# One RWKV-attention and MoE kernel, one reordering: where the inverses, the loads, x and the MoE pieces stand in a hand-written step table

## The chip, the cores and the metric

The kernel runs on one core of a Trainium2 chip. The metric is device time in microseconds (us), the median of several runs. Engines are named as in the profile: PE is the matrix engine (PEld its weight loads), DVE, ACT and POOL are the three vector-like engines, SP is the engine that here does nothing but issue DMAs (SPq is its queue). Each engine works through its own instructions strictly in the order of the program; between engines there are only semaphores.

## The reference

For 4 batches and 8 heads a state of 40x40 is carried over 768 time steps; its output is the input of a mixture layer:

```
for t in range(S):
    y[:, :, t] = einsum('bhd,bhde->bhe', rt, state)
    Sa = einsum('bhde,bhe->bhd', state, at)
    state = state * wt[:, :, None, :] - Sa (x) bt + vt (x) kt
x = y as (B, S, 320);  x_prev = x shifted by one time step
xk = mu_k * x + (1 - mu_k) * x_prev
xr = mu_r * x + (1 - mu_r) * x_prev
out = sigmoid(xr @ w_r) * (max(xk @ w_k, 0)**2 @ w_v)
```

All of it is float32. w_k is 320x1024, w_v 1024x320, w_r 320x320.

## The kernel before, in words

**Chunks.** Time is cut into 12 chunks of 64 (index k). Inside a chunk the recurrence becomes products, and one triangular system per head, whose 32x32 diagonal blocks are inverted on POOL. A chunk is done in two halves p = 0, 1 of 16 heads each; names such as `psc0` and `psc1` carry the half.

**What one chunk goes through.** `w` loads w, a, b, k of a half into the tile `wab` (L274); there are two such buffers, so a load waits until the transposes `pkt` of the half before the last are done with it. `Q` or `q` checks a half: ACT squares `wab` into `pe` (L289), an instruction that must wait for the load. The front (`F`, L300) then has four stages on DVE: two scans, two products into `az`, one product back into `wab`. `psc` (L322) makes the score matrix `sn` on PE, copied by ACT. `to` (L359) writes the blocks of `sn` to a DRAM scratch `tx` in 128-byte runs; `tl` (L373) loads them back as `ta` with one block per partition and inverts all of them on POOL (about 60 small instructions, L384 and L387) into `td`; `ts` (L364) stores `td` to the scratch `ty`; `tk` (L369) fetches `ty` back into `sn`. These trips to DRAM and back turn the layout around, each one must land before the next may be issued, and all are issued by SP. `tl` loads after `tx` has landed, `tk` after `ty` has.

**The chain of a chunk** (L403) has five stages on PE, `z T L U s`, each followed by ACT or DVE copies of its result `ch`; `T`, `L` and `U` need the fetched inverses in `sn`. `put`, `pmt`, `pgh`, `py` make the output y from the chain, from `r` and from `v` (`vr`, loaded by `r`, L397, two buffers; `vu`, loaded by `v`). `py` is copied by DVE into `xp`, and `x` (L512) sends `xp` by five DMAs into the tile `x` that the MoE layer reads.

**MoE work.** `Mix` (L115) cuts the layer of one chunk into 18 pieces: 8 products `ph` (relu, square and a split into two halves follow on ACT and DVE), 8 products `pv`, 2 products `pr` (each counted where its generator yields; the last two `pv` are the last two pieces). Before them stand 7 mixing steps on DVE and ACT (difference, three for xk, three for xr), the first four of which the first piece needs. `advance` (L527) issues the next piece; while a chunk's later pieces run, it may also issue mixing steps of the next chunk, if that chunk's `Mix` is already in the list, which happens at the end of its step (L635).

**Order.** The program is written out by hand (manual schedule): per chunk a step of 25 slots, `STEP` (L38). A slot's names are called from left to right; what they put off (`later`) comes at the end of that slot or of a following one. A name works on chunk k plus an offset (L568, L569): in step k, `psc`, `pkt`, `to`, `tl` belong to chunk k+2, `w` and `Q` to k+3, `ts` and `tk` to k+1, `r` and `v` to k+1, `x` to k. `M` is one MoE piece from step 1, slot 12 on (`MOE_FROM`); earlier it converts one of the 18 pieces of the weights from float64 bits (L222), which are loaded on ACT's queue. Slots are counted from 0. There are 19 slots with an `M` before.

**Head.** Ahead of step 0, chunks 0 and 1 (and half of 2) are brought through front, scores and inversion (L584 to L616).

In the step table the names from slot 14 on were, before:

```
"py0 tl", "M pgh1", "M pkt0", "M py1 w0 r0", "M pkt1 ts", "M w1 r1", "M", "M tk", "M x", "M Q0", "M F"
```

## Time and profile before

| | before |
|---|---|
| median of 3 runs (us) | 803.15 (802.92 to 803.17) |
| the profiled execution, own time (us) | 802.47 |
| its span in the profile (us) | 800.8 |
| busy share PE / DVE / ACT / POOL | 71% / 54% / 39% / 47% |
| mean granted clock of PE | 0.806 |
| DMA moved, mean rate | 71.15 MB, 89 GB/s |
| DMA packets, of them under 512 bytes | 120554, 96573 |

How to read the rows of the profile: a chain row is start, duration, what. A row of the timeline is start, duration, engine, line, operation, out<-in, shapes, count, and in brackets the idle time ahead of it and what ended it. A row of the windows is the stretch, its length, busy us (and instructions) of PE, PEld, DVE, ACT, POOL, then the granted clock of PE (1.00 is full), the mean busy share of the 16 DMA engines, and GB/s. An SPq row with a long duration is a DMA whose issue was itself held up.

### The profile page before, as it was taken

What the parts mean: (1) busy time and instruction counts of PE and PEld (TensorE: products, weight loads), DVE (VectorE), ACT (ScalarE), POOL (GpSimd) and SP (SyncE); (2) the same over time, 40 slices, a digit from 0 to 9 for tenths busy, and PEclk for the clock granted to TensorE, in tenths of its full rate; (3) what the DMA queues carried; (4) which work ended last, traced back from release to release, by engine and by line L of the source; (5) the groups of instructions that cost most, each with busy time, mean ns of one, the idle gap of its engine ahead of it and who ended that gap; (6) DMA issues with size and microseconds to landing.
All of it is one profiled execution on the core that took longest, in us unless ns stands there. A gap on an engine that the chain in (4) does not pass through costs nothing.

```text
span 800.8 us, 24776 instructions
## 1 busy us (share of the span) xinstructions
PE 571.1 (71%) x10658; PEld 516.7 (65%) x10658; DVE 433.5 (54%) x773; ACT 313.4 (39%) x793; POOL 373.5 (47%) x814
## 2 busy tenths in 40 slices
PE   1122086057979799797896794993994997988965
PEld 1122075046868688786786693883883886988965
DVE  7486677497466493663744544643653654232431
ACT  2122241143554464444443442442532533525333
POOL 4284787702823855858548248138038228200000
PEclk9999985555979789698698597597598598695979
DMA  4709536913625718348066066057048054160010
GB/s 122 152 13 188 125 72 148 187 40 69 132 50 133 128 35 182 53 108 154 23 129 113 23 134 110 21 121 138 6 100 156 9 102 74 30 102 10 10 33 20
DMA packets 120554, 71.15 MB, mean 89 GB/s; under 512 B 96573, under 2 KB 110869, under 8 KB 118149
## 3 DMA queue, kind: packets, MB, share of 16 engines
q1 hardware_dynamic: 118214, 63.74, 40.0%
q10 hardware_dynamic: 2223, 5.76, 2.9%
q8 instruction: 85, 1.39, 0.8%
q14 instruction: 32, 0.26, 0.1%
HBM read 52.98 MB, written 10.22 MB: 79 GB/s over the span
## 4 chain that ended last, share of the span: by engine, by line
PE 34%; DMA 28%; DVE 12%; SPq 9%; POOL 8%; issue 4%; ACT 3%; DVEq 0%; POOLq 0%; ACTq 0%
DMA ty<-td 10%; PE ph L112 9%; DMA ta<-tx 7%; PE pv L112 5%; SPq L371 4%; PE psc L333 4%; POOL td L387 3%; DMA x<-xp 3%; POOL ttmp L384 3%; PE ch L437 3%; PE ch L431 2%; PE ch L425 2%; SPq L521 2%; PE ch L419 2%; DMA wbuf<-in_w_v_dram 2%
## 5 line engine op out<-in xcount | busy, mean ns | idle before, releaser
L387 POOL TENSOR_TENSOR td<-td,ttmp 128x30 f32<-128x30 f32 (+4 forms) x360 | 165.3, 459 | 28.2
L384 POOL TENSOR_TENSOR ttmp<-ta,td 128x30 f32<-128x30 f32 (+4 forms) x360 | 161.2, 448 | 28.3
L112 PE MATMUL ph<-xk,wkh 120*128 120x256 f32 x480 | 115.5, 340 | 62.9 <-ACT xk L90 61.0
L112 PEld LDWEIGHTS ph<-xk,wkh 120*128 120x128 f32 x480 | 84.3, 223 | 72.7 <-ACT xk L90 64.7
L90 POOL TENSOR_TENSOR mc<-zs,pe 104x320 f32<-104x320 f32 x24 | 18.6, 790 | 172.1 <-DVE zs L90 171.9
L90 ACT ACTIVATE hf<-ph 128x256 f32<-128x256 f32 x96 | 36.9, 384 | 151.6 <-PE ph L112 150.9
L90 DVE TENSOR_TENSOR hl<-hf,hh 128x256 fp32r<-128x256 f32 x96 | 42.8, 445 | 92.0 <-ACT hh L90 91.7
L419 PE MATMUL ch<-zs,sn 32*32 32x40 f32 x768 | 29.9, 263 | 75.2 <-ACT zs L90 44.6
L378 POOL TENSOR_SCALAR_AFFINE_SELECT td<-ta 64x512 f32<-64x512 f32 x24 | 17.6, 732 | 139.5 <-DMA ta<-tx 139.2
L419 PEld LDWEIGHTS ch<-zs,sn 32*32 32x32 f32 x768 | 27.2, 164 | 78.6 <-ACT zs L90 44.9
L112 PE MATMUL ph<-xk,wkl 120*128 120x256 f32 x288 | 74.3, 316 | 0.1
L333 PE MATMUL psc<-az,wab 40*64 40x64 f32 x1536 | 37.9, 268 | 45.9 <-DVE wab L318 39.0
L112 PE MATMUL pv<-wvh,hh 128*128 128x320 f32 x192 | 69.5, 362 | 0.0
L333 PEld LDWEIGHTS psc<-az,wab 40*64 40x64 f32 x1536 | 34.1, 178 | 49.9 <-issue 48.8
L112 PE MATMUL pv<-wvh,hl 128*128 128x320 f32 x192 | 62.6, 326 | 0.0
L112 PE MATMUL pv<-wvl,hh 128*128 128x320 f32 x192 | 62.4, 325 | 0.0
L112 PEld LDWEIGHTS ph<-xk,wkl 120*128 120x128 f32 x288 | 57.2, 227 | 0.4 <-DMA xk<-xk 0.4
L90 DVE TENSOR_TENSOR az<-psc,mask 64x512 f32<-64x512 f32 x48 | 33.1, 689 | 41.5 <-PE psc L333 40.9
L90 ACT COPY vu<-ch 32x320 f32<-32x320 f32 x96 | 40.0, 416 | 27.5 <-PE ch L419 25.9
L139 DVE TENSOR_TENSOR diff<-x 120x256 f32<-120x256 f32 x36 | 16.6, 511 | 61.5 <-DMA x<-xp 61.4
L90 DVE TENSOR_TENSOR gh<-pgh,mask 128x512 f32<-128x512 f32 x48 | 30.9, 685 | 27.1 <-PE pgh L483 27.1
L306 DVE TENSOR_TENSOR_SCAN pe<-wab,first 104x520 f32<-104x520 f32 x24 | 31.6, 1318 | 23.8 <-ACT pe L90 19.7
(95 smaller groups left out, 1233.8 us busy)
## 6 DMA issues: line engine op xcount, KB each, us to landing
wab<-in_wab_dram SPq DMA_DIRECT2D x22, 835.7 KB
vr<-in_rvd_dram SPq DMA_DIRECT2D x24, 416.0 KB
ta<-tx SPq DMA_DIRECT2D x24, 256.0 KB
vu<-in_vt_dram SPq DMA_DIRECT2D x24, 256.0 KB
out_dram<-sig SPq DMA_DIRECT2D x48, 80.0 KB
tx<-sn SPq DMA_DIRECT2D x48, 64.0 KB
ty<-td SPq DMA_DIRECT2D x24, 128.0 KB
sn<-ty SPq DMA_DIRECT2D x48, 64.0 KB
```

The lines of the kernel that those rows point to most:

```text
L90: f(*args, **kw)
L112: nc.tensor.matmul(out, lhsT=left[i][g], rhs=right[j][g], start=start and k == 0, stop=stop and k == len(terms) - 1)
L139: nc.vector.tensor_tensor(out=d4[:, g], in0=x[:, g, :, 1:], in1=x[:, g, :, 0:C], op=ALU.subtract)
L306: nc.vector.tensor_tensor_scan(out=pe.rearrange("p x t -> p (x t)"), data0=w[:, 0:SP], data1=first, initial=0.0, op0=ALU.mult, op1=ALU.add)
L333: nc.tensor.matmul(to[64 * y:64 * y + 64, x], lhsT=kb[r0:r1, x, y], rhs=az[r0:r1, i, x], start=True, stop=True)
L371: nc.sync.dma_start(y, x)
L378: nc.gpsimd.affine_select(out=TD[h], in_=TA[h, i::2], compare_op=ALU.is_gt, fill=0.0, base=-i, pattern=[[-2, 16], [1, 32]], channel_multip ...
L384: nc.gpsimd.tensor_tensor(out=tmp, in0=TA[:, s:s + 1, s + 1:].broadcast_to([128, rows, n]), in1=TD[:, 0:rows, s:s + 1].broadcast_to([128, ...
L387: nc.gpsimd.tensor_tensor(out=TD[:, 0:rows, s + 1:], in0=TD[:, 0:rows, s + 1:], in1=tmp, op=ALU.subtract)
L419: mm(c3[a:a + 32, x], lhsT=sn[a:a + 32, x, 0:32], rhs=zs[a:a + 32, x], start=True, stop=True)
L425: mm(c3[a + 32:a + 64, x], lhsT=sn[a:a + 32, x, 32:64], rhs=vu[a:a + 32, i, x, 0:HD], start=False, stop=True, skip_group_check=True)
L437: mm(c3[r0:r1, x], lhsT=kt[:, i, x], rhs=vu[:, i, x, 0:HD], start=(x == 0), stop=True, skip_group_check=(x > 0))
```

## The change

Only the order of issue is changed; every instruction and every byte stays. In the step table:

- `ts` goes from slot 18 to 15 and `tk` from 21 to 18: both now stand ahead of the loads `w0` and `w1`, which go from 17 and 19 to 19 and 20.
- `x` goes from slot 22 to 19, behind `w0` and ahead of `w1`.
- `r0`, `r1` go from slots 17 and 19 of the step before (offset 1) to slots 1 and 3 of the chunk's own step (offset 0).
- `tl` goes from slot 14 to 13.
- `q1` goes from slot 1 to 3; the front of half 1 follows it in slots 4 to 7 instead of 3 to 6.
- Slot 18 loses its `M`: 18 slots with an `M` instead of 19.
- In the head, the loads of chunk 1 come behind `tri(0)`, `tri(1)` directly behind `tri_out(1)`, the load of `r` and `v` of chunk 0 by `load_rv` goes into step 0, store and fetch of chunk 0's inverses come between the two loads of chunk 2, and the eight weight pieces are spread 2, 2, 3, 1 instead of 1, 2, 2, 2, 1.

```
@@ -36,8 +36,8 @@
 MOE_FROM = (1, 12)
 
 STEP = [x.split() for x in (
-    "z0 z1 F", "M F q1", "T0 T1 F", "M pmt0 F", "L0 L1 F", "M pmt1 F", "U0 U1 F", "M psc0", "s0 s1", "M psc1", "M put0 to",
-    "M put1 v", "M pgh0", "M", "py0 tl", "M pgh1", "M pkt0", "M py1 w0 r0", "M pkt1 ts", "M w1 r1", "M", "M tk", "M x",
+    "z0 z1 F", "M F r0", "T0 T1 F", "M pmt0 q1 r1", "L0 L1 F", "M pmt1 F", "U0 U1 F", "M psc0 F", "s0 s1", "M psc1", "M put0 to",
+    "M put1 v", "M pgh0", "M tl", "py0", "M pgh1 ts", "M pkt0", "M py1", "pkt1 tk", "M w0 x", "M w1", "M", "M",
     "M Q0", "M F")]
 
 
@@ -565,7 +565,7 @@
                 psc(k, p)
 
             DO = dict(put=put, pmt=pmt, pgh=pgh, py=py)
-            AHEAD = dict(r=(1, load_rv), w=(3, load_wab), Q=(3, check), q=(2, check), psc=(2, scores), pkt=(2, pkt))
+            AHEAD = dict(r=(0, load_rv), w=(3, load_wab), Q=(3, check), q=(2, check), psc=(2, scores), pkt=(2, pkt))
             BOTH = dict(v=(1, load_v), to=(2, tri_out), tl=(2, tri), ts=(1, tri_store), tk=(1, tri_back), x=(0, send_x))
 
             def to_scores(k):
@@ -588,32 +588,30 @@
                     load_w(j, nc.sync)
                 to_scores(0)
                 tri_out(0)
-                load_wab(1, 0)
                 pkt(0, 1)
                 flush()
-                some_weights(1)
+                some_weights(2)
                 tri(0)
-                load_wab(1, 1)
+                for p in range(2):
+                    load_wab(1, p)
                 some_weights(2)
                 to_scores(1)
                 tri_out(1)
                 pkt(1, 1)
                 flush()
+                tri(1)
+                load_v(0)
                 load_wab(2, 0)
-                load_v(0)
-                for p in range(2):
-                    load_rv(0, p)
-                tri(1)
+                some_weights(3)
+                tri_store(0)
+                tri_back(0)
                 load_wab(2, 1)
                 for p in range(2):
-                    some_weights(2)
                     check(2, p)
                     flush()
                     for _ in range(2):
                         next(fronts[-1][2])
-                some_weights(1)
-                tri_store(0)
-                tri_back(0)
+                    some_weights(1 - p)
                 for k in range(NK):
                     chains = [chain(k, p) for p in range(2)]
                     for n, slot in enumerate(STEP):
```

## The prediction, on record before the changed kernel was run

> **What bounds the kernel now.** First the page of the profile: is one engine full all the time?

> ```profile
> span 800.8 us, 24776 instructions
> PE   1122086057979799797896794993994997988965
> PEclk9999985555979789698698597597598598695979
> ```

> From slice 9 on PE is nearly full twice and then half empty, about every 60 us, and the granted clock falls in the same rhythm. So a step is PE work, a hole, and a stretch at low clock behind the hole. The chain of waits and the timeline of PE give the beat; I take the start of stage T (L419) as the mark of a step and call it T(k). The first row below is T(2), from the timeline.

> ```profile
> 224.59 2.34 PE L419 MATMUL ch<-zs,sn 32*32 32x40 f32 x62 [0.38 <-DMA sn<-ty]
> ```

> ```profile
> 143.24 8.89 DMA wbuf<-in_w_v_dram
> 152.23 6.18 DMA wbuf<-in_w_v_dram
> ...
> 324.87 2.33 PE ch L419 x62
> ...
> 563.53 2.27 PE ch L419 x64
> ...
> 624.91 2.27 PE ch L419 x64
> ...
> 677.52 2.27 PE ch L419 x64
> ...
> 725.15 2.27 PE ch L419 x64
> ```

> The five later rows are T(4), T(8), T(9), T(10) and T(11). Steps 2 and 3 took (324.87 - 224.59) / 2 = 50.1 us each, step 8 took 61.4, steps 2 to 8 together (624.91 - 224.59) / 7 = 57.2 each, steps 9 and 10 52.6 and 47.6. The chain of waits through step 8 shows what stands in the hole:

> ```profile
> 583.07 1.09 PE psc L333 x64
> ...
> 588.45 5.64 DMA ta<-tx
> ...
> 598.60 8.91 DMA ty<-td
> ...
> 609.02 3.23 SPq L371
> ...
> 614.78 3.12 DMA x<-xp
> ...
> 617.92 1.44 DVE diff L139 x3
> ...
> 623.05 1.86 PE ph L112 x7
> ...
> 656.22 1.14 PE ph L112 x8
> ...
> 657.97 1.08 PE pv L112 x6
> ```

> The end runs through SP: scratch loaded, inverses stored, their fetch issued, x sent, mixed on DVE and ACT, and only then the first MoE piece of the new chunk, which stands in slot 1, ahead of T on PE. SP's own timeline shows the loads between:

> ```profile
> 596.63 0.35 SPq L277 DMA_DIRECT2D wab<-in_wab_dram  x1
> ...
> 601.44 3.40 SPq L277 DMA_DIRECT2D wab<-in_wab_dram  x1
> ...
> 607.59 4.66 SPq L371 DMA_DIRECT2D sn<-ty  x4
> ...
> 617.27 2.46 SPq L90 DMA_DIRECT2D out_dram<-sig  x4
> ```

> The windows show what the hole costs beyond itself:

> ```profile
> 608.00:612.00 4.00, 1.36 (x48) 1.24 (x44) 2.41 (x5) 0.85 (x2) 3.53 (x7) 1.00 0.94 164
> 612.00:616.00 4.00, 0.00 (x0) 0.00 (x0) 0.00 (x0) 0.00 (x0) 3.37 (x9) 0.59 1.03 147
> ...
> 636.00:640.00 4.00, 4.00 (x80) 3.58 (x79) 0.26 (x1) 2.19 (x6) 0.00 (x0) 0.50 0.00 0
> ...
> 644.00:648.00 4.00, 4.00 (x91) 3.48 (x89) 2.33 (x5) 2.34 (x6) 0.69 (x1) 1.00 0.20 32
> ```

> PE stops at about 609.4 and resumes at 623.05, a hole of 13.7 us; the clock is then 0.50 until after 640, some 17 us of work at half speed, that is 8 us more.

> **Part by part. 18 pieces a step.** A chunk's MoE layer has 18 pieces. Before, step 1 issued 12 from slot 12 on and left 6; each later step issues 19 and leaves one less, until step 7 leaves none and step 8 must begin slot 1 with a chunk whose x has only just been sent. After, step 1 issues 11 (slots 12, 13, 15 to 17, 19 to 24), 7 stay over, and stay 7: slots 1 to 11 work off the old chunk, the new one begins in slot 12, mixed long before. PE then reaches T without x. The price is at the end: 7 pieces more behind the last step, at 1.1 us (1.14 and 1.08 above) 7.8 us.

> **Store and fetch ahead of the loads, x too.** I count from the end of `psc1`, 583.07 + 1.09 = 584.16.

> ```profile
> wab<-in_wab_dram SPq DMA_DIRECT2D x22, 835.7 KB
> vr<-in_rvd_dram SPq DMA_DIRECT2D x24, 416.0 KB
> ```

> ```profile
> 600.00:604.00 4.00, 3.63 (x37) 3.18 (x35) 0.99 (x2) 2.19 (x6) 3.29 (x10) 1.00 0.84 197
> ```

> At 197 GB/s a `wab` load is 4.2 us, a `vr` load 2.1. `ta` was issued at +4.3; now the stores of the chunk whose last piece falls in slot 11 stand before it on SP (2.46), so +6.8, and it lands 5.64 later, +12.4. The store `ty` was landed at 598.60 + 8.91 = 607.51, 10.9 after the `wab` load was issued in front of it; without 6.3 of loads it is worth some 4.6 (an estimate from these rows), so it lands at +17.0, and the fetch, as many bytes, at +21.5. Then `w0` behind it in the DMA queues, +25.7; x, issued by about +24 and landing 3.1 later or behind `w0`, at +28; `w1` at +32. Before, fetch and x had both loads and both `r` ahead of them.

> PE needs no load to get from `psc1` to T: before, it issued 14 pieces and stage z and stood still at 609.4, +25.2; after, it is 13, z and one more in slot 1, the same. The fetch at +21.5 is no longer late. What is late next is `w0`: `Q0` in slot 23 makes ACT wait for it, and on ACT there are queued behind it the three passes of the piece in slot 24 and the copies of z.

> ```profile
> 606.08 0.72 ACT L90 ACTIVATE pe<-wab,limit 104x512 f32<-104x512 f32 x1
> ...
> 608.50 0.43 ACT L90 COPY zs<-ch 128x320 f32<-128x320 f32 x1 [1.61 <-PE ch L413]
> ```

> That is 0.72 + 3 x 0.4 + 0.43 = 2.3 behind +25.7: T at +28.0, PE idle 2.8 us instead of 13.7. From T to the end of `psc1`, step 4 had

> ```profile
> 342.29 1.16 PE L333 MATMUL psc<-az,wab 40*64 40x64 f32 x64
> ```

> and with T(4) of step 4 at 324.87 that is 18.6 us, partly at half clock, partly held by DVE. I take it whole, since x, at +28, again comes no sooner than T: a period of 28.0 + 18.6 = 46.6. In bounds: without the wait for `w0` and with 2 us of the low clock gone, 25.2 + 16.5 = 41.7; with T as late and the cold pace of step 8 (T 563.53 to 584.16, 20.6) and 2 us more of loads, 51.

> **V and r in their own step.** `r0`, `r1` now start behind `w1` and must land before `put` in slot 10, some 15 us after; 2 x 2.1 us of data. Cost nothing; without that cover, up to 4 us a step, which the upper bound has room for. The offset frees 832 KB from the crowded stretch.

> **tl, q1, F.** `tl` waits for the landing of `tx`, not for PE: nothing. `q1` waits on ACT for `w1` (+32) in slot 3, about when PE is there; the front of half 1 ends one slot later, still ahead of `psc1`. Zero to 1 us, inside the 18.6. `ts` in slot 15 needs POOL to be done:

> ```profile
> L387 POOL TENSOR_TENSOR td<-td,ttmp 128x30 f32<-128x30 f32 (+4 forms) x360 | 165.3, 459 | 28.2
> L384 POOL TENSOR_TENSOR ttmp<-ta,td 128x30 f32<-128x30 f32 (+4 forms) x360 | 161.2, 448 | 28.3
> ```

> (165.3 + 161.2) / 12 = 27 us, with its gaps about 31, from +12.4 of the step before: done at +44, asked for at 46.6 + 8. Ten us of cover.

> **Head and steps 0, 1.** The two waits of 8.89 and 6.18 above are weight loads of ACT's queue behind SP's loads of step 0; 832 KB (4.2 us) leave that stretch, and store and fetch go first. I take 10 of the 15, 5 for the head, where the same 832 KB leave and `ta` of chunk 1 no longer queues behind them, 5 for the hole ahead of T(2), less 2 for the weight piece that moves from step 0 to step 1: 18, between 5 and 25.

> **Sum.** Steps 2 to 8: 7 x (57.2 - 46.6) = 74.2. Step 9 has no `w` loads: 52.6 - (25.2 + 18.6) = 8.8. Step 10: no hole, so the low clock's 8. From T(11) to the end: 8 of the clock and some 6 of the wait for x and the mixing, now under the seven old pieces, less their 7.8: 6. Head 18. Together 115.0; 802.47 - 115.0 = 687.5, and the median lies 0.7 above the profiled execution: 688.

> **The rivals.** *Warm throughout.* If 2.8 us of idleness don't cost the clock, steps go to 41.7: 7 x 4.9 = 34 less, 654, and with the head at 25, 647. On the threshold:

> ```profile
> 388.00:392.00 4.00, 0.86 (x12) 0.62 (x7) 3.50 (x8) 2.26 (x6) 1.80 (x4) 0.85 0.15 38
> 392.00:396.00 4.00, 4.00 (x91) 3.66 (x92) 0.97 (x3) 2.02 (x5) 0.00 (x0) 0.50 0.24 58
> ```

> Here 3.1 us of idle PE cost the clock. I give the warm case 0.25. [...]

> *Cold and late.* The hole shrinks but stays, as in steps 2 and 3 now: 51 a step, 31 more, and the head at 5: 732. 0.2.

> *The store as slow as in the head, and the kernel slower.* In the head SP's timeline has

> ```profile
> 72.62 9.17 SPq L367 DMA_DIRECT2D ty<-td  x2
> 90.91 1.92 SPq L371 DMA_DIRECT2D sn<-ty  x4
> ```

> 18.3 us from the issue of the store to that of the fetch. Issued at +7.9, this gives +26.2 instead of +17.0; everything behind it on SP, `w0`, x and `w1`, shifts by 9.2, T to +37, and with 20.6 behind it the step is 58: 7 x 0.8 more, 7.8 for the pieces at the end, nothing won elsewhere: 815. It decides once the store lands 7 us later than I sum. Against it: in the head a `wab` load, two V loads and two `vr` loads stood ahead of that store beside `ta`, after the change only V, the output and `ta`. 0.04.

> *No gain.* The loads, later by what store and fetch take, hold the front so long that the hole only moves from the fetch to `Q0`; it needs T at about +36. 0.03.

> **The numbers.** Forecast 0.48, warm 0.25, cold and late 0.2, the last two 0.07. The range 647 to 738 takes the bounds of the steps and of the head (51 a step, the head at 5, 6 for steps 9 to the end). About 0.2% (1.6 us) is what a measurement can tell: faster 0.93, same 0.02, slower 0.05.

> **What would show it.** Right: T(k) every 45 to 48 us; the fetch landed before T, so that T is released by ACT and not by a DMA; the mixing of a chunk in slots 1 to 9 of the next step; PE holes under 4 us. Wrong: a hole over 5 us at T still, ACT waiting for `wab` much over 5 us a step, a wait of `ts` for POOL, or `psc1` held by DVE so that the step stays above 50.

## The result, and the profile after

| | before | after |
|---|---|---|
| median (us) | 803.16 (802.92 to 811.8, 4 runs) | 701.6 (698.51 to 709.03, 4 runs) |
| ratio to before | 1 | 0.87 (95% interval 0.8623 to 0.8777) |
| the profiled execution, own time | 802.47 | 709.03 |
| its span | 800.8 | 707.3 |
| mean granted clock of PE | 0.806 | 0.843 |

The kernel is 101.6 us faster by the medians, where 688 was forecast for a time of 701.6. The profiled execution of after is the slowest of its four, and the ratios leave out executions that stand out like this one, which the medians count; so the spans differ by 93.5 only, and the balance below is made on the spans, as the prediction's sum was.

The page of after, PE and its clock in 40 slices of the span:

```profile
PE   1103256605498999989989979899799799999994
PEclk9999996555578895895988968958959859999998
```

From slice 12 on PE is nearly full, where before had slices at 3 to 7 in nearly every step. The clock row has kept its rhythm: it still dips to 5 once a step. The starts of stage T in the timeline of PE, T(2), T(3), T(8) and T(9):

```profile
219.38 1.34 PE L419 MATMUL ch<-zs,sn 32*32 32x40 f32 x64
266.56 2.33 PE L419 MATMUL ch<-zs,sn 32*32 32x40 f32 x64 [3.05 <-ACT zs L90]
511.29 1.45 PE L419 MATMUL ch<-zs,sn 32*32 32x40 f32 x64 [3.65 <-ACT zs L90]
560.32 2.34 PE L419 MATMUL ch<-zs,sn 32*32 32x40 f32 x64 [3.65 <-ACT zs L90]
```

T is now released by ACT's copy of z and no longer by the fetch, and steps 2 to 8 take (560.32 - 219.38) / 7 = 48.7 us each (57.2 before, 46.6 forecast). The chain of waits of after through step 8:

```profile
530.95 1.09 PE psc L333 x64
...
550.41 7.48 DMA wab<-in_wab_dram
...
560.32 2.34 PE ch L419 x64
...
581.21 1.09 PE psc L333 x64
```

One load, `w0`, is left in the chain, where before had the load of the scratch, the store, the fetch's issue and x. `psc1` ends at 530.95 + 1.09 = 532.04; T follows at +28.3; the next `psc1` ends 22.0 behind T. SP's and ACT's timelines show the queue that the prediction summed:

```profile
542.99 1.28 SPq L367 DMA_DIRECT2D ty<-td  x2
548.41 1.90 SPq L371 DMA_DIRECT2D sn<-ty  x4
550.41 0.41 SPq L277 DMA_DIRECT2D wab<-in_wab_dram  x1
550.92 2.49 SPq L521 DMA_DIRECT2D x<-xp  x2
553.46 3.98 SPq L523 DMA_DIRECT2D x<-xp  x3
557.54 0.46 SPq L277 DMA_DIRECT2D wab<-in_wab_dram  x1
```

```profile
557.98 0.72 ACT L90 ACTIVATE pe<-wab,limit 104x512 f32<-104x512 f32 x1 [4.89 <-DMA wab<-in_wab_dram]
```

The store is issued, the fetch 5.4 us behind it, `w0` and x behind the fetch, and ACT has waited 4.89 us for `w0` when it starts at 557.98, 25.9 behind `psc1`. The windows of the same stretch (columns as in the section on the profile before):

```profile
556.00:560.00 4.00, 0.67 (x5) 0.41 (x3) 1.18 (x1) 1.96 (x6) 3.45 (x8) 1.00 0.89 151
560.00:564.00 4.00, 3.68 (x70) 3.59 (x71) 3.93 (x8) 2.26 (x6) 3.69 (x5) 0.52 0.79 192
...
576.00:580.00 4.00, 4.00 (x99) 3.80 (x95) 3.96 (x7) 0.99 (x2) 3.41 (x8) 0.50 0.02 4
580.00:584.00 4.00, 4.00 (x86) 3.48 (x86) 1.68 (x4) 1.25 (x3) 2.69 (x9) 0.92 0.03 7
```

3.65 us without PE work, and then PE is full and at half clock (0.52, later 0.50 in the rows) until after 580: nearly the whole way from T to `psc1`. That is where the forecast and the measurement part.

### The profile page after: what moved, and what is told of

It reads as the page before. It is cut to its first block, busy times and chain, and to the rows that moved or that the text cites. A ratio compares the mean times of both kernels' runs of the same rounds, so it can differ in the third digit from the quotient of the medians.

```text
span 707.3 us, 24797 instructions
## 1 busy us (share of the span) xinstructions
PE 541.4 (77%) x10658; PEld 496.2 (70%) x10658; DVE 440.4 (62%) x773; ACT 313.9 (44%) x793; POOL 396.5 (56%) x814
## 3 DMA queue, kind: packets, MB, share of 16 engines
q1 hardware_dynamic: 118214, 63.74, 42.6%
## 5 line engine op out<-in xcount | busy, mean ns | idle before, releaser
L387 POOL TENSOR_TENSOR td<-td,ttmp 128x30 f32<-128x30 f32 (+4 forms) x360 | 175.3, 487 | 28.2
L384 POOL TENSOR_TENSOR ttmp<-ta,td 128x30 f32<-128x30 f32 (+4 forms) x360 | 174.1, 484 | 28.3
L112 PE MATMUL ph<-xk,wkh 120*128 120x256 f32 x480 | 99.6, 306 | 6.2 <-ACT xk L90 5.2
L378 POOL TENSOR_SCALAR_AFFINE_SELECT td<-ta 64x512 f32<-64x512 f32 x24 | 18.4, 765 | 139.2 <-DMA ta<-tx 138.1
L90 DVE TENSOR_TENSOR hl<-hf,hh 128x256 fp32r<-128x256 f32 x96 | 43.2, 450 | 64.4 <-ACT hh L90 63.7
L112 PEld LDWEIGHTS ph<-xk,wkh 120*128 120x128 f32 x480 | 75.5, 200 | 10.8 <-ACT xk L90 5.7
L333 PE MATMUL psc<-az,wab 40*64 40x64 f32 x1536 | 39.4, 275 | 54.0 <-DVE wab L318 43.2
L333 PEld LDWEIGHTS psc<-az,wab 40*64 40x64 f32 x1536 | 35.6, 184 | 58.8 <-issue 55.7
L90 ACT ACTIVATE hf<-ph 128x256 f32<-128x256 f32 x96 | 36.6, 381 | 75.8 <-PE ph L112 75.5
L112 PE MATMUL pv<-wvh,hh 128*128 128x320 f32 x192 | 68.8, 358 | 1.8 <-issue 1.8
L419 PE MATMUL ch<-zs,sn 32*32 32x40 f32 x768 | 21.9, 229 | 62.6 <-ACT zs L90 62.6
L112 PE MATMUL ph<-xk,wkl 120*128 120x256 f32 x288 | 68.2, 292 | 0.0
L419 PEld LDWEIGHTS ch<-zs,sn 32*32 32x32 f32 x768 | 20.1, 134 | 65.3 <-ACT zs L90 64.7
L112 PE MATMUL pv<-wvh,hl 128*128 128x320 f32 x192 | 61.6, 321 | 0.0
L112 PE MATMUL pv<-wvl,hh 128*128 128x320 f32 x192 | 61.3, 319 | 0.0
L90 POOL TENSOR_TENSOR mc<-zs,pe 104x320 f32<-104x320 f32 x24 | 17.9, 767 | 58.7 <-DVE zs L90 58.0
L112 PEld LDWEIGHTS ph<-xk,wkl 120*128 120x128 f32 x288 | 50.7, 201 | 0.0
L90 DVE TENSOR_TENSOR az<-psc,mask 64x512 f32<-64x512 f32 x48 | 33.1, 689 | 22.3 <-PE psc L333 21.5
L90 ACT COPY vu<-ch 32x320 f32<-32x320 f32 x96 | 40.0, 416 | 12.9 <-PE ch L419 11.3
L112 PEld LDWEIGHTS pv<-wvh,hh 128*128 128x128 f32 x192 | 37.7, 197 | 6.0 <-issue 2.1
L90 ACT ACTIVATE hf<-hf 128x256 f32<-128x256 f32 x96 | 40.0, 417 | 3.1
## 6 DMA issues: line engine op xcount, KB each, us to landing
wab<-in_wab_dram SPq DMA_DIRECT2D x22, 835.7 KB
vr<-in_rvd_dram SPq DMA_DIRECT2D x24, 416.0 KB
```

The lines of the kernel that those rows point to most:

```text
L90: f(*args, **kw)
L112: nc.tensor.matmul(out, lhsT=left[i][g], rhs=right[j][g], start=start and k == 0, stop=stop and k == len(terms) - 1)
L333: nc.tensor.matmul(to[64 * y:64 * y + 64, x], lhsT=kb[r0:r1, x, y], rhs=az[r0:r1, i, x], start=True, stop=True)
L378: nc.gpsimd.affine_select(out=TD[h], in_=TA[h, i::2], compare_op=ALU.is_gt, fill=0.0, base=-i, pattern=[[-2, 16], [1, 32]], channel_multip ...
L384: nc.gpsimd.tensor_tensor(out=tmp, in0=TA[:, s:s + 1, s + 1:].broadcast_to([128, rows, n]), in1=TD[:, 0:rows, s:s + 1].broadcast_to([128, ...
L387: nc.gpsimd.tensor_tensor(out=TD[:, 0:rows, s + 1:], in0=TD[:, 0:rows, s + 1:], in1=tmp, op=ALU.subtract)
```

## The experiments

The theory after the result was: order and lag give the gain as summed; what is left in a step is the wait of ACT for `w0`, and the half clock that follows it. Rivals: the lag alone does it; the stretch from T to `psc1` is held by DVE and ACT whatever the clock. The table has each run's marks, read from its timeline of PE: T(2), the mean of steps 2 to 8, and its two parts (`psc1` to T, T to the end of `psc1`). Times are medians; each ratio is to the kernel before on the same chip. The marks come from one profiled execution of each run, and after's lies 7.4 us above its median, so half a microsecond a step between two rows (after, e6, e12) is not read as a difference.

| run | us | ratio (95%) | T(2) | step | psc1 to T | T to psc1 |
|---|---|---|---|---|---|---|
| before | 803.16 | 1 | 223.9 | 57.3 | 34.6 | 22.7 |
| after | 701.6 | 0.87 (0.862 to 0.878) | 219.4 | 48.7 | 28.2 | 20.5 |
| e1_lag_only | 739.35 | 0.915 (0.903 to 0.927) | 225.5 | 51.8 | 31.0 | 20.9 |
| e2_order_19 | 757.49 | 0.941 (0.933 to 0.949) | 218.5 | 52.0 | 30.5 | 21.5 |
| e6_r_next | 706.73 | 0.883 (0.873 to 0.892) | 221.5 | 48.2 | 27.5 | 20.8 |
| e7_x_late | 723.64 | 0.903 (0.893 to 0.913) | 220.6 | 51.0 | 27.7 | 23.2 |
| e12_x0_late | 704.84 | 0.871 (0.860 to 0.883) | 220.0 | 48.2 | 27.9 | 20.3 |
| e4_fill | 723.87 | 0.896 (0.887 to 0.904) | 223.7 | 48.5 | 32.7 | 15.8 |
| e5_fill16 | 699.02 | 0.873 (0.863 to 0.883) | 220.5 | 47.1 | 28.3 | 18.8 |
| e10_mix_late | 701.92 | 0.871 (0.863 to 0.879) | 216.6 | 46.9 | 28.8 | 18.1 |
| e3_w0_early | 671.27 | 0.834 (0.827 to 0.841) | 216.6 | 43.7 | 24.6 | 19.1 |
| e9_q1 | 668.98 | 0.830 (0.817 to 0.843) | 219.1 | 43.7 | 24.6 | 19.2 |
| e11_mix_late_w0 | 692.01 | 0.86 (0.852 to 0.868) | 216.1 | 45.5 | 27.1 | 18.4 |
| e13_best | 707.53 | 0.885 (0.880 to 0.889) | 217.1 | 47.4 | 29.6 | 17.8 |

**The change's two main parts, each alone.** e1 is the kernel before with 18 pieces a step (`pkt1 ts` without its `M`), e2 the changed kernel with 19.

```
e1: "M py1 w0 r0", "M pkt1 ts"  ->  "M py1 w0 r0", "pkt1 ts"
e2: "M py1", "pkt1 tk"          ->  "M py1", "M pkt1 tk"
```

> The kernel before, with nothing changed but the M taken out of slot 18. Theory order (store, fetch and x ahead of the loads are needed, 18 pieces alone only take x out of PE's way): every step from 2 to 8 becomes like steps 2 to 4 of before, which still held T until the fetch (50.8 us on average against 57.2), so 45 us less there, 5 in step 9, 14 in step 10 (as after the change), 9 in the tail: about 730 us; T is released by DMA sn<-ty with 4 to 5 us of idle PE ahead of it in every step, and the clock is still 0.50 behind it. Theory lag (the count of pieces is nearly all of it): about 705 us.

> The changed kernel with the M put back into slot 18, so 19 pieces a step. Theory order: as the changed kernel (48.7 us a step) until the leftover is used up about step 7; from then on slot 1 needs the x just sent (landed 28 us behind psc1), then 5 us of difference and mixing and 2 of the piece: T at +35.5 instead of +28, 7 to 8 us more in steps 8 and 9 and about 12 in step 10, some 5 less in the tail: about 722 us. Theory lag: without the lag nearly nothing of the gain is left in the late steps and the fetch still holds the early ones: 740 or more.

The lag alone is worth some 69 us on this chip (808.83 - 739.35), the order alone some 51; 0.915 x 0.941 = 0.861, against 0.87 for both. So they add up within the intervals; neither is the other's condition. e1 came out above both of its expectations (730 or 705); its steps, 51.8, are near the 50.8 of the order theory. e2 came out in the range of the lag theory (740 or more for 757.49), but not by its mechanism: the fetch no longer holds the early steps. With the lag alone T still waits for the late fetch:

```profile
PE ch L419 <- DMA sn<-ty: 53.5, 16, 6.8
```

(waits of e1: us in all, times, longest.) With the order alone the fetch is early, but T to `psc1` grows from 17.2 at T(2) to 28.0 at T(7), as the new chunk's first piece moves forward by one place a step and PE waits for its mixed input `xk` (43.3 us over the run, 5.2 in after), and steps 7 and 8 take 62.8 and 54.4.

**w0 earlier.** The prediction named the wait of ACT for `w0` as what is late next. e3 issues `w0` two slots earlier, ahead of the fetch:

```
"M py1", "pkt1 tk", "M w0 x"  ->  "M py1 w0", "pkt1 tk", "M x"
```

> The changed kernel with w0 moved from slot 19 to slot 17, ahead of the fetch on SP, behind the store. Theory Q0 (the hole that is left ahead of T is ACT waiting in Q0 for the load w0, landed 26 us behind psc1): w0 now moves while the store lands and arrives at about +20.5, before slot 23; ACT does not wait for wab in slot 23, the hole falls from 3.6 us to under 1, the clock stays at 1.00 behind T, and a step takes 44 instead of 48.7: 670 us. Rival (the fetch or DVE sets T as well, w0 only comes first by chance): 697 to 704 us, with T released by the fetch.

671.27, as the theory had it. SP's timeline of e3:

```profile
463.96 1.28 SPq L367 DMA_DIRECT2D ty<-td  x2
466.46 0.82 SPq L277 DMA_DIRECT2D wab<-in_wab_dram  x1
469.08 1.91 SPq L371 DMA_DIRECT2D sn<-ty  x4
```

`w0` stands in the 5 us in which the store is landing, and the fetch follows the store at 5.1, no later than in after (5.4). T comes 24.6 behind `psc1`, with no idle time ahead of it. But T to `psc1` has only fallen from 20.5 to 19.1, though T's hole is gone; PE now waits further on, ahead of stage U (L431), which shows in the waits of e3:

```profile
PE ch L431 <- ACT zs L90: 22.5, 8, 4.3
```

**The hole ahead of T filled.** Products of the identity in slot 1 of the changed kernel keep PE busy while ACT waits. The first try had 34 of them in every step, the second 16, in steps 0 to 8 alone.

```
+ def fill(n):  p = ps("sw", "fill")
+     for _ in range(n): nc.tensor.matmul(p[:, 0:128], lhsT=ident, rhs=ident, start=True, stop=True)
"M F r0"  ->  "M D F r0"      (D: fill(34); e5: fill(16) if k + 3 < NK)
```

> The changed kernel with 34 products of the identity with itself added on PE in slot 1, right ahead of T; nobody reads them, nothing else is changed. They last 3.7 us at full clock, as long as the hole. Theory idle (the low clock behind T is the price of the 3.6 us of idle PE): the granted clock stays at 1.00 behind T, T to the end of psc1 falls from 20.7 to about 18.4 (then held by DVE): some 15 us less, 686 us. Rival (the small products of T, L and U let the clock fall by themselves, or DVE holds psc1 anyway): clock 0.50 as before the filling, or no gain: 700 us or a little more.

> The changed kernel with 16 identity products on PE in slot 1, ahead of T, in steps 0 to 8 alone (those that have a wab load). The filler of 34 products before took 7.75 us (32 instructions are half of that, some 3.7 us), as long as PE's hole ahead of T. Idle theory (the hole costs the clock, the clock costs the stretch from T to the end of psc1): T stays 28 behind psc1, the clock stays at 1.00, T to psc1 falls from 20.7 to 15 to 16, steps 2 to 8 from 48.7 to about 43.5, some 35 us less: 665 to 672. Rival, DVE or ACT hold psc1 18 us behind T whatever the clock: 688 to 695. Rival, products so small don't hold the clock: 700 or more.

In e4 the filler was twice as long as meant: a product of 128x128 in float32 is two instructions in the trace, 0.114 us each.

```profile
507.75 7.75 PE L560 MATMUL fill<-ident 128*128 128x128 f32 x68
```

T came 4.5 us later, and the filler cost time where there was no hole to fill (step 9 52.3, step 10 41.4, T(2) 4.3 later): 723.87. But the clock stayed at 1.00 around T in most steps, and T to `psc1` was 15.8. That looks like the idle theory. e5 has the right length, T where it was (28.3), no idle time ahead of it and the clock at 1.00 there, and still 699.02: 0.873 against 0.87. The idle theory (665 to 672) is out. The time lies between the ranges of the two rivals; the mark of 18.8 is that of the first, DVE or ACT, but not "whatever the clock", as PE's timeline of e5 shows:

```profile
357.17 3.73 PE L560 MATMUL fill<-ident 128*128 128x128 f32 x32
360.83 1.34 PE L419 MATMUL ch<-zs,sn 32*32 32x40 f32 x64
...
369.88 1.63 PE L431 MATMUL ch<-zs,sn 32*32 32x40 f32 x64 [3.49 <-ACT zs L90]
```

The hole has moved from T to U, 3.49 us, and the clock goes with it: the 64 products of `psc` at 373.88 take 1.99 us, as they do in after at 0.50 (574.86), and 1.16 at 1.00. Its DVE and ACT show why the copy of zs for U is late:

```profile
362.15 1.78 DVE L139 TENSOR_TENSOR diff<-x 120x256 f32<-120x256 f32 x3
363.85 1.72 DVE L316 TENSOR_TENSOR az<-wab,pe 40x512 f32<-40x512 f32 x2
365.61 1.35 DVE L318 TENSOR_TENSOR wab<-wab 104x1024 f32<-104x1024 f32 x1
366.87 0.47 DVE L147 SCALAR_TENSOR_TENSOR xm<-diff,muk,x 120x256 f32<-120x256 f32 x1
```

```profile
367.38 0.41 ACT L90 CAST xk<-xm 120x256 fp32r<-120x256 f32 x1 [2.73 <-DVE xm L147]
367.69 0.85 ACT L90 COPY mk<-pmt 40x320 f32<-40x320 f32 x2
368.56 0.72 ACT L90 ACTIVATE pe<-wab,limit 104x512 f32<-104x512 f32 x1
...
369.40 0.75 ACT L90 COPY zs<-ch 128x320 f32<-128x320 f32 x2
```

The new chunk's mixing is threaded between the stages of the front on DVE; ACT waits for its first result (a cast), and the copy that U needs stands behind that cast, two copies and the check of `q1`. In after this is hidden: there T comes at the same time, but PE runs at 0.50 behind it and reaches U no earlier, 9.2 to 9.8 us behind T in steps 3 to 8 against 9.05 in this step of e5.

**The mixing out of that stretch.** e10 lets 12 old pieces reach into the next step instead of 7, so that the new chunk's mixing falls in slots 11 to 15.

```
MOE_FROM = (1, 12)                 ->  (1, 19)
4 if mixes[0].last_ph else 1       ->  4 if mixes[0].last_ph else 0
```

> The changed kernel with MOE_FROM (1, 19) instead of (1, 12), so that 12 old pieces instead of 7 reach into the next step, and the new chunk's difference waits for the last ph as its other mixing steps do (4 if last_ph else 0). Its mixing then stands on DVE behind psc1, in slots 11 to 15, instead of between the front's stages in slots 1 to 7. The DVE theory (the filler run left the step as it was: from the landing of w0 to psc1 the time is DVE's front with the mixing between its stages and the copies that ACT holds behind it): 4.5 us of mixing on DVE leave that stretch, 3 to 4 us a step in steps 2 to 8, less 5.5 us for 5 more pieces at the end: 676 to 686. Rival, the clock alone sets the stretch: psc1 stays 20 to 22 behind T, and the total rises by the 5.5: 704 to 710.

701.92, above the 676 to 686 of the DVE theory and just under the other. The steps are not alike, though: 42.6, 48.2, 48.4, 44.4, 49.6, 45.5, 49.6. PE's timeline in step 5 and in step 8:

```profile
355.92 1.34 PE L419 MATMUL ch<-zs,sn 32*32 32x40 f32 x64 [1.53 <-ACT zs L90]
363.19 1.34 PE L431 MATMUL ch<-zs,sn 32*32 32x40 f32 x64 [1.73 <-ACT zs L90]
...
369.19 1.16 PE L333 MATMUL psc<-az,wab 40*64 40x64 f32 x64
```

```profile
495.43 2.21 PE L419 MATMUL ch<-zs,sn 32*32 32x40 f32 x64 [1.54 <-ACT zs L90]
505.13 2.34 PE L431 MATMUL ch<-zs,sn 32*32 32x40 f32 x64
...
515.52 1.41 PE L333 MATMUL psc<-az,wab 40*64 40x64 f32 x64
```

The same instructions take 1.34 us in the one and up to 2.34 in the other, and T to `psc1` 14.4 and 21.5. So there are two bounds on this stretch. Where the clock is down for 17 or 20 us behind T, it lasts 20 to 22 us, mixing or not. At full clock and without the mixing it lasts 12.6 to 14.4 (steps 2 and 5 of e10). With the mixing, PE reaches U early, stands still there (3.49 us in the step of e5 above) and goes cold. Taking away one leaves the other, which is why neither e5 nor e10 moved the total. What e10 won in the steps (1.8 us each) it paid back behind step 8: T(9) to the end is 156.9 us against 147.0 in after, for five more pieces, which the expectation had at 5.5.

**Both, on the faster kernel.** e11 is e3 with the edit of e10. e9 is e3 with `q1` a slot later; e13 adds to e9 a lag of 8 pieces, MOE_FROM (1, 13), with the mixing begun two pieces behind the last `ph`.

```
e9:  "M pmt0 q1 r1", "L0 L1 F", ... "s0 s1"  ->  "M pmt0 r1", "L0 L1 q1", ... "s0 s1 F"
```

> The kernel with w0 in slot 17 (671.3) and q1 one slot later, in slot 4, its front in slots 5 to 8. There a hole of 2.3 us stands ahead of U, where ACT's copy of zs is queued behind a cast of the mixing, two copies and the check of q1, and some 7 us behind it run at 0.50 to 0.60. If taking the check (0.9 us) out of that queue closes enough of the hole for the clock to hold, steps go from 43.7 to 40 to 41 and the total to 645 to 652. If the cast that waits for DVE keeps the hole over 1.5 us and the clock falls anyway: 666 to 671. If the later front holds psc1 by a slot, 2 us a step: 680 to 686.

> The same edit on the kernel with w0 in slot 17 (671.3). The DVE theory: 43.7 a step to about 40, where PE is nearly full at full clock (40.5 to 41 us busy a step there, at a mean clock of 0.92), less 5.5 at the end: 646 to 656. Rival, the clock alone: 674 to 680.

> The kernel with w0 in slot 17 and q1 in slot 4 (669), MOE_FROM (1, 13), and the new chunk's mixing begun only two pieces behind the last ph, so in slots 9 to 12, behind psc1's front on DVE, with the output store still ahead of the next inverses on SP. If it is two bounds that take turns (the mixing between the front's stages on DVE, and the cold clock behind the hole ahead of U that the mixing makes), both go: psc1 14 to 16 us behind T at full clock, 24 to 25 from psc1 to T as with w0 in slot 17, steps of 39 to 41 against 44, less one more piece at the end: 640 to 652. Rival, w1 lands so late that q1 alone keeps the hole ahead of U or psc1: 43 to 44 a step, 660 to 670. Rival, what the runs with 12 old pieces showed (the output store in front of x and w1): 680 to 692; it needs that store behind the store of the inverses, and it stands ahead of it here.

e9 is e3 again, as its second expectation had it (668.98, 666 to 671): the hole ahead of U was 2.3 to 2.9 us in e3 and is 1.7 to 2.3 here, and the clock went all the same (`psc` takes 1.99 us at 315.57, behind a hole of 1.73, and 1.16 at 322.13). e11 is slower than e3, and above both of its expectations (692.01, 680 at most). The chunk's output leaves later when its last piece does, and SP's and ACT's timelines show where that puts it:

```profile
430.03 1.92 SPq L371 DMA_DIRECT2D sn<-ty  x4
432.04 5.28 SPq L90 DMA_DIRECT2D out_dram<-sig  x4
...
442.24 0.46 SPq L277 DMA_DIRECT2D wab<-in_wab_dram  x1
```

```profile
450.37 0.72 ACT L90 ACTIVATE pe<-wab,limit 104x512 f32<-104x512 f32 x1 [5.11 <-DMA wab<-in_wab_dram]
```

The output store holds SP for 5.28 us ahead of x and `w1`; `q1` waits 5.11 us for `w1`, with U's copy behind it on ACT (step 7, the step with the longest hole ahead of U, 4.75). e13 keeps that store early and misses by more, 707.53 against 640 to 652, and above its rivals too. Its mixing, pushed into slots 9 to 12, now comes too late for the first piece of the new chunk (PE idle some 1.5 us for `xk` in most steps, and the clock is down again behind that, from 477.5 to 484.4 for one: a pair of `ph` products takes 0.80 us at 482.62 and 0.50 at 485.64), and PE stalls in the middle of U:

```profile
362.56 1.19 PE L431 MATMUL ch<-zs,sn 32*32 32x40 f32 x54 [2.16 <-issue]
410.00 1.94 PE L431 MATMUL ch<-zs,sn 32*32 32x40 f32 x50 [2.78 <-issue]
...
508.43 1.67 PE L431 MATMUL ch<-zs,sn 32*32 32x40 f32 x42 [2.50 <-issue]
```

"issue" is time for which the profile shows no wait. T to `psc1` did fall, to 17.8, but `psc1` to T rose to 29.6. The fastest version found is e3 or e9, which a measurement can't tell apart.

**The smaller moves.** e6 puts r back (offset 1, `r0` behind `w0`, `r1` behind `w1`, chunk 0 in the head), e7 puts x back into slot 22, e12 sends x of chunk 0 alone in slot 24 of step 0.

> The changed kernel with r back at its old place (offset 1, r0 behind w0 and r1 behind w1, chunk 0 in the head). The prediction took r's move at nothing by itself. If T waits for w0 alone (w0 is issued ahead of r0) and x and w1 have slack: 700 to 706. Rival, the 832 KB in the crowded stretch count in full (4.2 us a step at 197 GB/s, behind which w1 and so q1 and psc1 come later): 725 to 735. In the head, T(2) no more than 5 us later.

> The changed kernel with x back in slot 22, behind w1. If the 7 old pieces cover x (the new chunk's first piece stands in slot 12 of the next step), steps 2 to 8 stay at 48.7, and only the tail pays some 3 pieces (3 us): 702 to 706. Rival: the subtraction that waits for x stands on DVE in slot 1 ahead of the front and of the chain's copies, so x landing 5 us later holds T to psc1 by up to 5 us in each of 7 steps: 730 to 740.

> The changed kernel with x of chunk 0 alone sent in slot 24 of step 0 instead of slot 19 (its first reader is the MoE layer in step 1, slot 12). In step 0 ACT waits 12.1 us for a DMA of x before it may issue a weight load, and the copies of z are queued behind. If that wait is what kept steps 0 and 1 at 62 and 60: T(1) from 159 to 150 to 153, T(2) 6 to 10 us earlier, 692 to 696. Rival, the weight loads share the DMA engines with w1 and r of step 1 and land late anyway: T(2) within 2 us, 699 to 704.

r's place makes no difference that these runs can tell (the intervals overlap, the steps are 48.2 and 48.7). x's place does: 723.64, between the two expectations, and by the rival's mechanism. DVE's timeline of e7:

```profile
376.90 1.62 DVE L139 TENSOR_TENSOR diff<-x 120x256 f32<-120x256 f32 x3 [2.97 <-DMA x<-xp]
378.44 1.68 DVE L316 TENSOR_TENSOR az<-wab,pe 40x512 f32<-40x512 f32 x2
```

The subtraction stands in slot 1 ahead of the front's third stage and waits for x, 22.7 us over the run; T to `psc1` grows by 2.7. e12 changed nothing: T(2) is within 1 us, where its rival had said 2. In after ACT waited 12.09 us for a DMA of x before it could go on with the weights of step 0, in e12 it waits longer for another:

```profile
148.04 0.55 ACT L231 ACTIVATE wbuf<-wbuf 128x384 f32<-128x384 f32 x1 [12.09 <-DMA x<-xp]
```

```profile
149.33 0.54 ACT L231 ACTIVATE wbuf<-wbuf 128x384 f32<-128x384 f32 x1 [15.87 <-DMA wab<-in_wab_dram]
```

The weight load is no reader of either. What ties it to a DMA of x in after and to one of `wab` in e12 was not shown, and what the tie costs is open, since no run took it away.

## Why the prediction was right, and where it was wrong

- **psc1 to T, 28.0:** right. Seven steps give 27.7 to 29.4, mean 28.2, and in step 8 the sum's marks hold within 1.5 us: `w0` landed at +25.9 (25.7 forecast), the fetch issued at +16.4 for a forecast landing of the store at +17.0, x issued by +25.4 (24). Part of that is luck: the store was issued at +11.0, ahead of the landing of `ta` (+12.4) that the sum put in front of it and without a wait for POOL, and took 5.4 us to the fetch, where 4.6 was estimated. The next late thing was named rightly, and e3 shows that it was: with `w0` earlier the same part is 24.6.
- **T to psc1, 18.6: the term that failed.** It measures 20.5; with 0.2 from the other part a step is 2.1 longer than forecast, 48.7 and so just above the 45 to 48 that were to show it right, and seven steps make 14.2 us of the miss. The 18.6 was read too short: the row at 324.87 (x62) is not the first of stage T, which starts at 324.11, so that step of before took 19.3. And it ran "partly at half clock", 12 us of it; in after the clock falls at each T from T(3) to T(9), for 17 or 20 us, and the stretch behind takes 20.6 to 22.1 (T(5) alone: 10 us, and 17.9). The upper bound had said so ("the cold pace of step 8, 20.6"). What the number was made of was not seen: with the clock held at T, the same stretch doesn't fall to 16.5 but stops at 18.8 (e5), since DVE's mixing and ACT's queue hold U, and the clock falls there.
- **Head and steps 0 and 1, 18: failed.** T(2) came 4.5 us earlier (223.9 to 219.4): 1.3 up to T(0), 0.6 in step 0, 2.6 in step 1. The term that failed was "10 of the 15" us that ACT waits for its weight loads, since 832 KB leave that stretch. They didn't: SP isn't paced by the slots, and `r0`, `r1` of step 1 have nothing to wait for, so SP issued them right behind `w1`, while ACT's waits ahead of its weight work were 12.09 us and then 6.12, no less than the 15 of before. That is 13.5 us of the miss; what would shorten these waits stays open (e6 and e12 didn't). From SP's timeline of after:

```profile
145.20 0.49 SPq L277 DMA_DIRECT2D wab<-in_wab_dram  x1
146.03 2.20 SPq L400 DMA_DIRECT2D vr<-in_rvd_dram  x2
```

- **18 pieces, 7 over:** right; T no longer waits for x, the mixing of the new chunk is in slots 1 to 9, and e1 and e2 show lag and order as separate gains. Its price is higher than 1.1 us a piece: five more cost 9.9 in e10.
- **x ahead:** right that x comes no sooner than T; three slots later it costs 22 us (e7), by way of DVE. **r in its own step:** "cost nothing" holds within the measurement (e6).
- **Steps 9, 10 and the tail:** 52.6 to 46.6, 6.1 for 8.8; 47.6 to 33.9, 13.7 for 8; and 75.7 to 66.5, 9.2 for 6. The excess belongs to the lag: with the lag alone (e1) step 10 is 33.8 and the tail 65.6, with the order alone (e2) 46.6 and 73.8. The sum had counted only the half clock in step 10.
- **The sum:** 115.0 - 14.2 (steps 2 to 8) - 13.5 (head) - 2.7 (step 9) + 5.7 (step 10) + 3.2 (tail) = 93.5, the difference of the spans. That the total is off by less than its terms is luck: 30.4 us of misses one way, 8.9 the other.
- **The rivals:** not warm throughout: holes of 3.05 to 3.96 us ahead of T cost the clock, and in e10 holes of 1.3 to 1.5 us did too. Nor does a full PE bring it back at once: in after PE is full at 0.50 from 560.32 until after 580, some 20 us. Not cold and late: 48.7, not 51. The store never took the head's 18 us.

## What to carry to other kernels

When a hole is closed, find the next one on the same engine before pricing the gain: here the hole went from T to U, and with it the half clock, so filling it bought nothing, while issuing the load that T waited for two slots earlier bought 30 us. A lag between two streams in one program moves everything that the later stream does, its output stores and its vector work too; look at where each lands in the queues, because 12 old pieces instead of 7 put a store in front of the loads (5.28 us of SP in e11). And SP, which only issues DMAs here, was paced by its waits and not by the slots of the program, so an early slot for a load that waits for nothing meant "right behind the last one" (`vr` issued at 146.03 behind `wab` at 145.20, in after).

## What the runs showed of the hardware

```profile
362.19:365.60 3.41, 0.48 (x26) 0.48 (x28) 1.91 (x3) 2.55 (x7) 3.02 (x6) 1.00 0.93 166
365.60:375.84 10.24, 10.24 (x172) 9.46 (x168) 8.06 (x12) 5.58 (x14) 9.38 (x12) 0.50 0.65 143
375.84:379.25 3.41, 3.41 (x126) 3.10 (x122) 3.36 (x6) 2.49 (x7) 3.02 (x6) 1.00 0.04 12
```

- T to `psc1` follows that count in after: 17.9 us with 3 beats behind T (step 5), 20.6 to 20.8 with 5 (steps 4, 6, 8), 22.1 with 6 (steps 3, 7). So it is the clock that sets this stretch there. In e3, behind the hole ahead of U, it is shorter: products are slow from 224.4 to 230.9 and from 442.2 to 452.7, some 2 and 3 beats. What decides at which beat the clock comes back wasn't tried.
- Holes of the same length did not cost the same: 1.53 us ahead of T in step 5 of e10, and PE stayed at 1.00 through a second hole of 1.73 (T and U take 1.34 us each behind them); 1.54 us in step 8, and it ran at 0.50 from 496 until after 515 (T 2.21 us, U 2.34); and 1.28 us in step 9 cost the clock too (U 2.67). So the length alone does not decide it in these traces; what does was not shown.
- The stalls without a shown wait in e13 fall into the same group of 64 products, in each step four products later in it (54 and 50 are left behind the stall in steps 5 and 6, 42 in step 8). That looks like a constant distance in PE's instruction stream, slightly longer than a step, and not like a wait for another engine. What it is stays open.
